# Chunks 0 and 1 of the second mixture by Strassen's products, their first weight combined straight from its loads

## The chip, the cores and the metric

The kernel runs on one core of one Trainium2 chip. The metric is device microseconds of one execution. TensorE (PE) multiplies, VectorE (DVE), ScalarE (ACT) and GpSimd (POOL) do the elementwise work, and SyncE (SP) issues every DMA.

## The reference, cut to what matters

An attention feeds a first channel mixture ("moe"), and that feeds a second one ("moe2"). The change concerns the way from the first mixture to the second and the second's hidden layer:

```python
B, H, S, D = 4, 8, 576, 64                     # 2304 rows of 512 in what follows
x = attention(q, k, v)                         # a band of the scores, plus one on sums of 4 rows
xk, xr = mu_k * x + (1 - mu_k) * x_prev, mu_r * x + (1 - mu_r) * x_prev
k = np.maximum(xk @ w_k, 0.0)                  # 512 x 1024
x1 = sigmoid(xr @ w_r) * (k * k @ w_v)
mu = np.mean(x1, axis=-1, keepdims=True)
var = np.mean((x1 - mu) ** 2, axis=-1, keepdims=True)
xn = (x1 - mu) / np.sqrt(var + 1e-06) * g_ln
out = x1 + np.maximum(xn @ w_ch1, 0.0) @ w_ch2 # 512 x 2048, 2048 x 512
```

The weights arrive as 64-bit floats.

## The kernel before

**Chunks and splits.** The 2304 rows are six chunks of C = 384. Each operand of a large product is split into a high and a low part (`float32r`), and a product is three matmuls (`mm3`, lines 776 to 779): high by high, high by low, low by high.

**Order.** Nothing is issued as it is written down. Each operation is added to a `Plan` with its engine or engines, an assumed cost, a priority and what it reads and writes. `Plan.order` (line 121) is a list scheduler: of what is ready it takes the operation that can start earliest on its engine, and among equals the one with the lowest priority number. Buffers of one tag (a `Buf` with `bufs` slots) are given out in a fixed order of turns, by the first priority of each buffer. The dictionary `PRM` holds the numbers from which the priorities are made. The result is one fixed order for each engine, and SP's order is that of the DMAs.

**Weights.** `load_f32` (line 381) loads a 128x512 piece of 64-bit floats into `w64` (two slots) and makes 32-bit floats of it with two ScalarE operations (lines 393, 395) and two VectorE operations (lines 400, 404) in `wf` (two slots). `load_split` (line 408) adds the copy to the high part and the difference for the low part (line 418). There are 52 such pieces, 16 of `w_ch1` and 16 of `w_ch2` among them.

**Attention.** `attention` (line 451) handles a batch and two heads at a time, 16 units in all; `vsum4` (line 587) makes the sums of four rows of v for twelve of them, by two additions on POOL or one `tensor_reduce` on VectorE. The attention's pool `at` is closed when its last operation is done (`close_att`, `gate`), and the pool `w1tiles` takes its place. Its results stand transposed in `xT[b]`, one for each batch, tag `xT` of `xpool` with two slots.

**First mixture.** For each chunk `prep` (line 784) makes the split xr and xk from `xT` through two slots of `tmu`; `moe_r`, `moe_k` and `accumulate` do the products (tiles `psr`, `psk`, `psv`), and `moe_x` stores x1 to `x1_dram`. Chunk 5's last prep is the last reader of `xT[3]`.

**Second mixture.** Chunks 0 and 1 are done one after the other in the plain form. `c_prep` (line 937) takes one chunk: load x1 into `x1t` (tag `xT` again), statistics, normalised rows `z` stored to `z_dram` one tile of 128 rows after the other, fetched back block by block into `zb` (tag `tmu`, four DMAs each), transposed on VectorE, scaled and split. Chunk 0's is placed in chunk 5 of the first mixture, chunk 1's inside chunk 0's second mixture. `c_h` (line 983) makes the hidden layer from the 16 split pieces of `w_ch1`, which stay in SBUF, four kt by three matmuls for each of 16 f.

Chunks 2 and 3, and 4 and 5, are done as pairs by Strassen's seven products over a 2x2 cut of the rows (the two chunks), of the inner dimension (kt 0, 1 against 2, 3) and of the hidden dimension (f against f + 8). `w1_combine` (line 892) makes the combinations of `w_ch1` from the split pieces and stores them in `s_dram`. `m2_prep` (line 1016) does for both chunks of a pair what `c_prep` does for one, into two buffers `raw0` and `raw1` of the tag `xT`; `m2_split` (line 1095) subtracts and splits for the products in the order of `SEQ`; `m2_product` (line 1125) fetches a combination (`sa`) and runs 2 x 3 matmuls; `m2_h` (line 1153) does the seven for one f, and `m2_acc` the second layer, six row tiles by two pieces of `w_ch2`.

```python
SEQ = (1, 6, 2, 5, 7, 3, 4)
ROW = {1: 0, 6: 5, 2: 2, 5: 1, 7: 4, 3: 3, 4: 2}
for q, (kt, c) in enumerate(((j, 2 * p), (j, 2 * p + 1), (j + 2, 2 * p), (j + 2, 2 * p + 1))):  # m2_prep
minus(C, s(4), s(3), s(1), prio, [(b, 3), (b, 1)], [(b, 4)])
minus(C, s(1), s(1), s(0), prio, [(b, 0)], [(b, 1)])
minus(C, s(5), s(3), s(1), prio, [(b, 3), (b, 1)], [(b, 5)])
```

So product 1 reads row 0 of both `raw` buffers, and product 6 row 5, which is made from rows 0, 1 and 3 of each.

Of the kernel before, what the change touches and what calls it, by code (L numbers as in the profile page):

```python
# [253 lines left out]
def c_pool(n):  # L254
    return 0.2 + n * 0.0028


def c_dma(nbytes, run=2048):

    return nbytes / run * {128: 16, 256: 26, 1024: 72, 1536: 90, 2048: 95, 4096: 220}[run] / 16e3  # L260
# [3 lines left out]
def attn_moe_kernel(  # L264
# [186 lines left out]
    def attention(n, T0, TL):  # L451
# [421 lines left out]

    w1pool = [None]
    w1tiles = lambda: w1pool[0]
    W1, W2 = {}, {}
# [14 lines left out]

    def w1_combine(g, j, prio):

        a = {"11": W1[g, j], "21": W1[g + 2, j], "22": W1[g + 2, j + 2], "12": W1[g, j + 2]}
        to = lambda i, x: s_dram[4 * g:4 * g + 4, SEQ.index(i), :, j, x].rearrange("f p c -> p f c")
        for i, x in ((1, "11"), (2, "12"), (4, "22")):
            for h in range(2):
                b = a[x][h]
                add("SP", c_dma(P * 2048), prio, lambda i=i, h=h, b=b: nc.sync.dma_start(
                    out=to(i, h), in_=b().bitcast(F32).rearrange("p (f c) -> p f c", c=P)),  # L900
                    r=[b], w=[(sd, (i, g, j, h))], lat=2.2)

        def join(x, tag, n):
            hi, lo = a[x]
            o = Buf(wk, [P, 512], F32, tag, n, f"a{x}")
            minus(512, o, lambda: hi().bitcast(F32), lambda: lo().bitcast(F32), prio, [hi, lo], [o], ALU.add)
            return o

        def put(i, src):
            t = Buf(wk, [P, 4, 2, P], F32R, "w64", 2, f"s{i}")  # L910
            part = lambda x: (lambda: t()[:, :, x])
            split(512, part(0), part(1), lambda: src().rearrange("p (f c) -> p f c", c=P), prio, [src], [t])
            add("SP", c_dma(P * 4096), prio, lambda: nc.sync.dma_start(
                out=s_dram[4 * g:4 * g + 4, SEQ.index(i), :, j].rearrange("f p x c -> p f x c"), in_=t().bitcast(F32)),
                r=[t], w=[(sd, (i, g, j, h)) for h in range(2)], lat=2.2)

        a21 = join("21", "wf", 2)
        s1 = join("22", "wf", 2)
        minus(512, s1, a21, s1, prio, [a21], [s1], ALU.add)
        put(5, s1)  # L920
        a11 = join("11", "r", 3)
        minus(512, a21, a11, a21, prio, [a11], [a21])
        put(7, a21)
        minus(512, a11, s1, a11, prio, [s1], [a11])
        put(6, a11)
        a12 = join("12", "wf", 2)
        minus(512, a12, a12, a11, prio, [a11], [a12])
        put(3, a12)

    def c_load(c, prio):  # L930
# [3 lines left out]
            r=[(x1d, c)], w=[(t, i) for i in range(TT)], lat=2.2)  # L934
        return t

    def c_prep(c, x1t, prio):
        mv = Buf(wk, [P, TT, 2], F32, "mv", 2)
        for t in range(TT):
            bs = Buf(wk, [P, 6], F32, "bs", 2)  # L940
# [456 lines left out]
```

## Time and profile before

| | us |
|---|---|
| median of 3 runs (lowest, highest) | 781.41 (779.31, 782.21) |
| profiled execution | 778.78 |
| its span, first to last instruction | 776.8 |
| PE, DVE, ACT, POOL busy | 762.0, 521.8, 396.9, 55.7 |

Attention and first mixture run interleaved until some 265 us, the rest of the first mixture until 383 us, the plain second mixture of chunks 0 and 1 until 517 us, and the two pairs after it to the end. In the rows an operation stands with its line, engine, `out<-in` and shapes; in a timeline the first two numbers are its start and its length in us, and what stands in brackets is how long the engine sat idle before it and what ended that.

### The profile page before, as it was taken

To read this page: it belongs to the slowest core of one execution; us is meant where nothing else is said; L and a number is where in the kernel's file an instruction comes from. 1 tells how busy PE (TensorE), PEld (TensorE's weight loads), DVE (VectorE), ACT (ScalarE), POOL (GpSimd) and SP (SyncE) were. 2 spreads that over 40 slices of the span, in tenths; PEclk is the share of its full clock that TensorE was granted. 3 is DMA by queue.
4 is the path that set the end of the run, shared out by engine and by line. 5 is a ranking of instruction groups with operands and counts; after the bars stand their busy time and mean duration, and the time that the engine had idled before them with its cause. 6 is when DMAs were issued, how large, how long until landed. Compare 5 with 4: busy or idle time off the path is not lost.

```text
span 776.8 us, 15370 instructions
## 1 busy us (share of the span) xinstructions
PE 762.0 (98%) x5859; PEld 659.8 (85%) x5859; DVE 521.8 (67%) x1032; ACT 396.9 (51%) x909; POOL 55.7 (7%) x107
## 2 busy tenths in 40 slices
PE   8999999999999999999999999999999999999998
PEld 5777787878888797988989999999988898989986
DVE  5998999976966669868787857947553365233233
ACT  5888987854756788859655324512331131111110
POOL 2001112211110000000000000200000020000000
PEclk9999999999999999999999999999999999999999
DMA  8999594753320234536564897968763437434422
GB/s 182 183 181 184 150 208 101 140 107 60 86 38 22 96 108 141 173 107 176 161 179 180 245 326 226 285 218 267 189 163 110 121 110 254 153 109 121 123 68 81
DMA packets 182452, 119.10 MB, mean 153 GB/s; under 512 B 125536, under 2 KB 150252, under 8 KB 182380
## 3 DMA queue, kind: packets, MB, share of 16 engines
q1 hardware_dynamic: 182380, 118.14, 56.3%
q8 instruction: 46, 0.75, 0.4%
q14 instruction: 26, 0.21, 0.1%
HBM read 89.26 MB, written 28.84 MB: 152 GB/s over the span
## 4 chain that ended last, share of the span: by engine, by line
PE 86%; DVE 5%; ACT 3%; DMA 3%; issue 1%; SPq 0%; POOL 0%; DVEq 0%; ACTq 0%; POOLq 0%
PE pso L778 9%; PE pso L779 9%; PE pso L777 9%; PE psh L779 8%; PE psh L778 8%; PE psh L777 8%; PE psk L777 4%; PE psv L777 4%; PE psk L779 4%; PE psk L778 4%; PE psv L779 4%; PE psv L778 4%; PE psr L777 2%; PE sc L628 2%; PE pv L747 2%; PE psr L779 2%
## 5 line engine op out<-in xcount | busy, mean ns | idle before, releaser
L778 PE MATMUL psh<-xn,sa 128*128 128x384 f32 x224 | 75.7, 338 | 0.0
L777 PE MATMUL psh<-xn,sa 128*128 128x384 f32 x224 | 75.6, 338 | 0.0
L779 PE MATMUL psh<-xn,sa 128*128 128x384 f32 x224 | 75.5, 337 | 0.0
L777 PEld LDWEIGHTS psh<-xn,sa 128*128 128x128 f32 x224 | 42.1, 188 | 4.5 <-DVE t L1172 0.2
L778 PEld LDWEIGHTS psh<-xn,sa 128*128 128x128 f32 x224 | 42.1, 188 | 3.9
L377 ACT ACTIVATE c22h<-t 128x384 fp32r<-128x384 f32 x16 | 8.4, 526 | 71.4 <-DVE t L1172 71.4
L393 ACT ACTIVATE wf<-w 128x512 f32<-128x512 f32 x52 | 34.8, 669 | 17.0 <-DMA w<-in_moe_w_k_dram 6.2
L400 DVE SCALAR_TENSOR_TENSOR wf<-wf,w 128x512 uint32<-128x512 uint32 x52 | 35.7, 686 | 10.5 <-ACT w L395 9.6
L779 PEld LDWEIGHTS psh<-xn,sa 128*128 128x128 f32 x224 | 42.0, 188 | 0.0
L377 ACT ACTIVATE hh<-psh 128x384 fp32r<-128x384 f32 x32 | 15.7, 492 | 48.8 <-PE psh L779 46.9
L404 DVE SCALAR_TENSOR_TENSOR wf<-w,wf 128x512 uint32<-128x512 uint32 x52 | 35.5, 682 | 0.4
L842 DVE TENSOR_TENSOR kl<-kr,kh 128x384 fp32r<-128x384 f32 x42 | 23.3, 554 | 17.1 <-ACT kr L841 17.1
L395 ACT ACTIVATE w<-w 128x512 uint32<-128x512 uint8 x52 | 34.6, 666 | 0.0
L377 ACT ACTIVATE kr<-psk 128x384 f32<-128x384 f32 x45 | 22.0, 488 | 24.6 <-PE psk L779 21.0
L801 DVE SCALAR_TENSOR_TENSOR tmu<-xT,oms,tmu 128x384 f32<-128x384 f32 (+1 forms) x64 | 31.6, 518 | 0.6 <-ACT tmu L795 0.4
L795 ACT ACTIVATE tmu<-xT,vecs 128x192 f32<-128x192 f32 (+1 forms) x55 | 27.2, 522 | 6.0 <-DVE xrl L805 2.8
L995 DVE SCALAR_TENSOR_TENSOR hl<-psh,hh 128x384 fp32r<-128x384 f32 x32 | 17.7, 555 | 17.1 <-ACT hh L377 16.8
L377 ACT ACTIVATE c11h<-psh 128x384 fp32r<-128x384 f32 x16 | 7.9, 492 | 40.5 <-PE psh L779 40.5
L1149 DVE SCALAR_TENSOR_TENSOR c11l<-psh,c11h 128x384 fp32r<-128x384 f32 x16 | 8.9, 554 | 26.2 <-ACT c11h L377 26.2
L593 DVE TENSOR_REDUCE vd<-v 72x256 f32<-72x1024 f32 x11 | 21.8, 1982 | 6.0 <-PE up L717 6.0
L839 ACT ACTIVATE kh<-kr 128x384 fp32r<-128x384 f32 x48 | 25.0, 521 | 0.8
L431 PE MATMUL warm<-isum,identb 128*128 128x304 bf16 x130 | 23.0, 315 | 1.8 <-DVE identb L324 1.8
(779 smaller groups left out, 2309.0 us busy)
## 6 DMA issues: line engine op xcount, KB each, us to landing
sa<-s_dram SPq DMA_DIRECT2D x112, 256.0 KB
w<-in_moe_w_ch_dram SPq DMA_DIRECT2D x32, 512.0 KB
s_dram<-s SPq DMA_DIRECT2D x16, 512.0 KB
vw<-in_v_dram SPq DMA_DIRECT2D x62, 96.0 KB
x_dram<-r SPq DMA_DIRECT2D x18, 256.0 KB
x1t<-x_dram SPq DMA_DIRECT2D x6, 768.0 KB
z_dram<-x1t SPq DMA_DIRECT2D x18, 256.0 KB
zb<-z_dram SPq DMA_DIRECT2D x96, 48.0 KB
```

The lines of the kernel that those rows point to most:

```text
L377: return [("ACT", c_act(n, True), lambda: nc.scalar.activation(dst(), src(), AF.Relu), False), ("DVE", c_dve(n), lambda: nc.vector.tensor_ ...
L393: add("ACT", c_act(512), prio, lambda: nc.scalar.activation(f(), w64().bitcast(F32)[:, :, 1], AF.Abs, scale=2.0 ** -112), r=[w64], w=[f])
L395: add("ACT", c_act(512), prio, lambda: nc.scalar.activation(w64()[:, :, 0], w64().bitcast(U8).rearrange("p a (b c) -> p a b c", c=4)[:, :, ...
L400: lambda: nc.vector.scalar_tensor_tensor(fu(), fu(), 3, w64()[:, :, 0], op0=ALU.logical_shift_left, op1=ALU.bitwise_or),
L404: lambda: nc.vector.scalar_tensor_tensor(fu(), w64()[:, :, 1], 0x80000000, fu(), op0=ALU.bitwise_and, op1=ALU.bitwise_or),
L777: nc.tensor.matmul(ps, lh, rh, start=start, stop=False, skip_group_check=more)
L778: nc.tensor.matmul(ps, lh, rl, start=False, stop=False, skip_group_check=more)
L779: nc.tensor.matmul(ps, ll, rh, start=False, stop=stop, skip_group_check=more)
L795: add([("ACT", c_act(n, ap=1), lambda t=t, o=o, n=n, cur=cur, kt=kt: nc.scalar.mul(t()[:, o:o + n], cur(), mu[:, kt:kt + 1]), False), ("DV ...
L801: lambda t=t, o=o, n=n, prv=prv, kt=kt: nc.vector.scalar_tensor_tensor(t()[:, o:o + n], prv(), om[:, kt:kt + 1], t()[:, o:o + n], op0=ALU. ...
L839: add("ACT", c_act(C), prio, lambda: nc.scalar.activation(kh(), kr(), AF.Square), r=[kr], w=[kh])
L842: add(either(C, lambda e: e.tensor_tensor(kl(), kr(), kh().bitcast(F32), op=ALU.subtract)), 0, prio, None, r=[kr, kh], w=[kl])
```

## The change

Chunks 0 and 1 become pair 0 of the same form as the other two; `c_load`, `c_prep`, `c_h` and `c_out` go. `m2_prep` and `m2_split` for pair 0 stand in chunk 5 of the first mixture. `w_ch1` no longer stays in SBUF as split pieces: `w1_combine` loads 32-bit pieces, and makes and stores all seven combinations, high and low parts apart. Twelve of the 16 pieces are converted early (`w1_convert`, with priorities in chunks 1 and 2), stored to `w1_dram` and loaded from there; the last four are converted in `w1_combine`. All of `w1_combine` waits for the end of the attention and has priorities in chunk 4. The sums of v get a two-step form on VectorE as well. `w_ch2`'s pieces come in the order 0, 8, 1, 9 and so on. All priorities in `PRM` change; new ones (`ra`, `rb`, `rx`) shift single chunks.

```diff
 PRM = dict(
...
-    d0=190.212, d1=76.663, d2=272.12, d3=80.108, d4=165.422, d5=790.372,
+    d0=235.165, d1=108.349, d2=260.708, d3=463.399, d4=581.694, d5=82886.056,
...
+    wc=10.079, wcs=106.739, wcg=-39.001, p0l=11.872, p0=2.352, p0s=3.263, p0n=7.723, dp=684.729,
+    ra4=-5.44, rb4=10.116, ne=12, we=52.842, wes=25.704, wel=6.378,
...
         def vsum4():
-            def vsum():
-                nc.gpsimd.tensor_tensor(v4()[:, :, 0:2, :], v4()[:, :, 0:2, :], v4()[:, :, 2:4, :], op=ALU.add)
-                nc.gpsimd.tensor_tensor(vd(), v4()[:, :, 0, :], v4()[:, :, 1, :], op=ALU.add)
+            def vsum(e):
+                e.tensor_tensor(v4()[:, :, 0:2, :], v4()[:, :, 0:2, :], v4()[:, :, 2:4, :], op=ALU.add)
+                e.tensor_tensor(vd(), v4()[:, :, 0, :], v4()[:, :, 1, :], op=ALU.add)
-            add([("POOL", c_pool(512) + c_pool(256), vsum, True),
-                 ("DVE", c_dve(1024), lambda: nc.vector.tensor_reduce(
-                     vd(), v4().rearrange("p a r d -> p a d r"), axis=AX.X, op=ALU.add), False)],
+            add([("POOL", c_pool(512) + c_pool(256), lambda: vsum(nc.gpsimd), True),
+                 ("DVE", c_dve(512) + c_dve(256), lambda: vsum(nc.vector), True)],
                 0, pr(0.3), None, r=[v4], w=[v4, vd])
...
+    def w1_parts(g, j):
+        return ("21", g + 2, j), ("22", g + 2, j + 2), ("11", g, j), ("12", g, j + 2)
+    def w1_convert(fo, d, prio):
+        w1_early.add((fo, d))
+        f = Buf(wk, [P, 512], F32, "wf", 2)
+        load_f32(w_ch1[d * P:(d + 1) * P, 512 * fo:512 * fo + 512], f, prio)
+        add("SP", c_dma(P * 2048), prio, lambda: nc.sync.dma_start(out=w1_dram[fo, d], in_=f()),
+            r=[f], w=[(w1d, (fo, d))], lat=2.2)
     def w1_combine(g, j, prio):
-        a = {"11": W1[g, j], "21": W1[g + 2, j], "22": W1[g + 2, j + 2], "12": W1[g, j + 2]}
...
+        for x, fo, d in w1_parts(g, j):
+            a[x] = Buf(w1tiles, [P, 512], F32, "wa", 4, f"a{x}")
+            if (fo, d) in w1_early:
+                add("SP", c_dma(P * 2048), prio - PRM["wel"], lambda x=x, fo=fo, d=d: nc.sync.dma_start(
+                    out=a[x](), in_=w1_dram[fo, d]), r=[(w1d, (fo, d))], w=[a[x]], lat=2.2)
+            else:
+                load_f32(w_ch1[d * P:(d + 1) * P, 512 * fo:512 * fo + 512], a[x], prio)
         def put(i, src):
...
+                tag = f"sa{n_put[0] % 7 + 1}" if g == 0 else f"alt{n_put[1] % 3}"
...
+            add(copy(512, hi, src), 0, prio, None, r=[src], w=[hi])
+            add(either(512, lambda e: e.tensor_tensor(lo(), src(), hi().bitcast(F32), op=ALU.subtract)), 0, prio, None,
+                r=[src, hi], w=[lo])
+            for x, b in enumerate(parts):
+                add("SP", c_dma(P * 2048, 512), prio, lambda x=x, b=b: nc.sync.dma_start(
+                    out=s_dram[4 * g:4 * g + 4, SEQ.index(i), :, j, x].rearrange("f p c -> p f c"),
+                    in_=b().bitcast(F32).rearrange("p (f c) -> p f c", c=P)), r=[b], w=[(sd, (i, g, j, x))], lat=2.2)
...
+        if c == 1:
+            for i in range(PRM["ne"]):
+                g, j = divmod(i // 4, 2)
+                w1_convert(*w1_parts(g, j)[i % 4][1:], start[1] + PRM["we"] + PRM["wes"] * i)
...
-                    W1[g, kt] = load_split(w_ch1[kt * P:(kt + 1) * P, 512 * g:512 * g + 512], 0, f"w1{g}{kt}",
-                                           start[4] + PRM["w1"] + PRM["w1s"] * (4 * g + kt), pool=w1tiles)
+            for i in range(4):
+                w1_combine(i // 2, i % 2, start[4] + PRM["wc"] + PRM["wcs"] * i + PRM["wcg"] * (i > 1))
...
             elif f == PRM["x1"]:
-                x1t[0] = c_load(0, st(TT * 1.33 + 2 * f))
-                xn[0] = c_prep(0, x1t[0], st(TT * 1.33 + 2 * f + PRM["x1d"]))
+                raws = m2_prep(0, T_2 - PRM["p0l"], T_2 - PRM["p0"])
+                xp = m2_split(0, raws, lambda n: T_2 - PRM["p0s"] + PRM["p0n"] * n)
...
-    for c in range(2):
...
-        for f in range(F2 + 2):
-            if f < F2:
-                hs[f] = c_h(c, f, xn[c], st(2 * f))
...
-    for p in range(1, NP):
+    for p in range(NP):
```

## Rows read from the trace of the kernel before

**Rows 1.** The page, busy time of each engine.

```profile
PE 762.0 (98%) x5859; PEld 659.8 (85%) x5859; DVE 521.8 (67%) x1032; ACT 396.9 (51%) x909; POOL 55.7 (7%) x107
```

**Rows 2.** The page, the chain that ended last, by engine.

```profile
PE 86%; DVE 5%; ACT 3%; DMA 3%; issue 1%; SPq 0%; POOL 0%; DVEq 0%; ACTq 0%; POOLq 0%
```

**Rows 3.** Busy time by stage: stretch, its length, then us busy and instructions.

```profile
core 0: us, PE busy (x) PEld busy (x) DVE busy (x) ACT busy (x) POOL busy (x), PEclk, DMA share, GB/s
0.00:60.00 60.00, 54.96 (x961) 41.36 (x964) 48.71 (x108) 43.87 (x120) 9.98 (x38) 1.00 0.93 182
60.00:131.00 71.00, 67.25 (x782) 55.01 (x771) 67.90 (x133) 61.22 (x151) 10.45 (x19) 0.98 0.69 162
131.00:262.00 131.00, 130.05 (x1605) 107.46 (x1604) 101.19 (x210) 86.67 (x234) 18.19 (x37) 1.00 0.38 77
262.00:343.00 81.00, 80.36 (x401) 70.43 (x400) 58.02 (x119) 64.62 (x132) 1.02 (x1) 1.00 0.42 136
343.00:383.00 40.00, 39.41 (x194) 34.70 (x194) 32.21 (x63) 32.05 (x64) 1.02 (x1) 1.00 0.55 158
```

**Rows 4.** Timeline of PE at the start of the plain second mixture and its end.

```profile
381.37 0.39 PE L777 MATMUL psv<-wv5h,kh 128*128 128x512 f32 x1
...
383.45 0.34 PE L777 MATMUL psh<-xnh,w100h 128*128 128x384 f32 x1
...
385.53 0.34 PE L777 MATMUL psh<-xnh,w100h 128*128 128x384 f32 x1
...
517.04 0.34 PE L777 MATMUL psh<-xn,sa 128*128 128x384 f32 x1
```

**Rows 5.** Groups by line and shape: count, us busy, mean ns, idle before.

```profile
L400 DVE SCALAR_TENSOR_TENSOR wf<-wf,w 128x512 uint32<-128x512 uint32 x52 | 35.7, 686 | 10.5 <-ACT w L395 9.6 <-issue 0.3
L393 ACT ACTIVATE wf<-w 128x512 f32<-128x512 f32 x52 | 34.8, 669 | 17.0 <-DMA w<-in_moe_w_k_dram 6.2 <-DMA w<-in_moe_w_ch_dram 5.5 <-DMA w<-in_moe_w_r_dram 3.0
L593 DVE TENSOR_REDUCE vd<-v 72x256 f32<-72x1024 f32 x11 | 21.8, 1982 | 6.0 <-PE up L717 6.0
L890 DVE TENSOR_TENSOR a<-a,a 128x512 f32<-128x512 f32 x14 | 9.6, 684 | 0.2
```

**Rows 6.** Timelines of ACT, DVE and SP where chunk 1's x1t follows chunk 5's prep.

```profile
338.90 0.52 ACT L373 CAST xkh<-tmu 128x384 fp32r<-128x384 f32 x1 [2.58 <-PE psk L779]
...
347.59 0.62 DVE L801 SCALAR_TENSOR_TENSOR tmu<-xT,oms,tmu 128x384 f32<-128x384 f32 x1 [0.20 <-ACT tmu L795]
...
348.23 0.38 SPq L932 DMA_DIRECT2D x1t<-x_dram  x1
...
353.43 1.28 DVE L941 BATCH_NORM_STATS2 bs<-x1t 128x6 f32<-128x512 f32 x2
```

**Rows 7.** Timelines of DVE and SP, the preparation of chunks 4 and 5.

```profile
525.42 1.25 DVE L1027 BATCH_NORM_STATS2 bs<-x1t 128x6 f32<-128x512 f32 x2
...
529.44 0.54 DVE L1049 TENSOR_SCALAR x1t<-x1t,mv,rstd 128x512 f32<-128x512 f32 x1
...
535.75 0.54 DVE L1049 TENSOR_SCALAR x1t<-x1t,mv,rstd 128x512 f32<-128x512 f32 x1
...
544.65 0.54 DVE L1049 TENSOR_SCALAR x1t<-x1t,mv,rstd 128x512 f32<-128x512 f32 x1
...
545.79 0.57 DVE L1065 STREAM_TRANSPOSE raw<-zb 128x384 f32<-128x384 f32 x1
...
547.65 0.56 DVE L1117 TENSOR_TENSOR xn<-raw,xn 128x384 fp32r<-128x384 f32 x1 [0.34 <-ACT xn L373]
...
549.66 4.99 SPq L1061 DMA_DIRECT2D zb<-z_dram  x8
...
554.75 0.89 SPq L1128 DMA_DIRECT2D sa<-s_dram  x2
...
561.55 0.57 DVE L1065 STREAM_TRANSPOSE raw<-zb 128x384 f32<-128x384 f32 x1
...
571.20 0.58 DVE L1065 STREAM_TRANSPOSE raw<-zb 128x384 f32<-128x384 f32 x1 [0.89 <-DMA zb<-z_dram]
```

**Rows 8.** Busy time and granted clock (PEclk) of a stretch after two waits of PE.

```profile
91.00:95.00 4.00, 3.63 (x19) 3.08 (x20) 3.48 (x10) 3.57 (x10) 1.27 (x2) 0.57 0.36 123
```

More of the change, by code (lines that the diff above doesn't have):

```diff
@@ L875, in attn_moe_kernel @@
     w1tiles = lambda: w1pool[0]
-    W1, W2 = {}, {}
+    W2 = {}
     F4 = F2 // 2
@@ L983, in c_h @@
-    def c_h(c, f, xn, prio):
-        hi, lo = xn
-        ps = Buf(ps_k, [P, 512], F32, "pk", 2, "psh")
-        g, o = divmod(f * P, 512)
-        for kt in range(KT):
-            wh, wl = W1[g, kt]
-            add("PE", MM, prio, lambda kt=kt, wh=wh, wl=wl: mm3(
-                ps()[:, :C], wh()[:, o:o + P], wl()[:, o:o + P], hi()[:, kt], lo()[:, kt], kt == 0, kt == KT - 1),
-                r=[(hi, kt), (lo, kt), wh, wl], w=[ps])
-        hh = Buf(wk, [P, C], F32R, "kh", 3, "hh")
-        hl = Buf(wk, [P, C], F32R, "kl", 3, "hl")
-        add(relu(C, hh, lambda: ps()[:, :C]), 0, prio, None, r=[ps], w=[hh])
-        add("DVE", c_dve(C), prio, lambda: nc.vector.scalar_tensor_tensor(
-            hl(), ps()[:, :C], 0.0, hh().bitcast(F32), op0=ALU.max, op1=ALU.subtract), r=[ps, hh], w=[hl])
-        return hh, hl
@@ L999, in c_out @@
-    def c_out(c, pv, load_prio, prio):
-        for t in range(TT):
-            row = c * C + t * P
-            if c == 0:
-                add("DVE", c_dve(512), prio, lambda t=t: nc.vector.tensor_tensor(
-                    x1t[0]()[:, t], pv[t](), x1t[0]()[:, t], op=ALU.add), r=[pv[t]], w=[(x1t[0], t)])
-                add("SP", c_dma(P * 2048), prio, lambda t=t, row=row: nc.sync.dma_start(
-                    out=outf[row:row + P, :], in_=x1t[0]()[:, t]), r=[(x1t[0], t)], lat=2.2)
-                continue
-            x = Buf(wk, [P, 512], F32, "r", 3, "res")
-            add("SP", c_dma(P * 2048), load_prio, lambda row=row, x=x: nc.sync.dma_start(
-                out=x(), in_=x1_dram[row:row + P, :]), r=[(x1d, c)], w=[x], lat=2.2)
-            add("DVE", c_dve(512), prio, lambda t=t, x=x: nc.vector.tensor_tensor(x(), pv[t](), x(), op=ALU.add),
-                r=[pv[t]], w=[x])
-            add("SP", c_dma(P * 2048), prio, lambda row=row, x=x: nc.sync.dma_start(
-                out=outf[row:row + P, :], in_=x()), r=[x], lat=2.2)
+    n_put = [0, 0]
@@ L1253, in attn_moe_kernel @@
     xk[0] = prep(0, "k", prep_prio(T_M + PRM["xk"], PRM["xks"]))
-    x1t, xn = {}, {}
     glb = mub
@@ L1308, in attn_moe_kernel @@
-                xn[0] = c_prep(0, x1t[0], st(TT * 1.33 + 2 * f + PRM["x1d"]))
-        moe_x(c, pvs[c], rr, T + DU + 1)
-    for i, f in enumerate(range(4, F2)):
-        W2[f] = load_split(w_ch2[f * P:(f + 1) * P, :], f, f"w2{f}", T_2 + PRM["w2"] + PRM["w2s"] * i)
-    for kt in range(KT):
-        W1[3, kt] = load_split(w_ch1[kt * P:(kt + 1) * P, 1536:2048], 16 + kt, f"w13{kt}", T_2 + PRM["w13"] + PRM["w13s"] * kt)
-    converted = [b.writer[None] for w in (W1, W2) for hl in w.values() for b in hl]
@@ L1315, in attn_moe_kernel @@
-    for c in range(2):
-        T = T_2 + D2 * c
-        st = lambda i: T + D2 * i / (2 * F2)
-        pv = [Buf(ps_v, [P, 512], F32, f"pv{t}", 1, f"pso{t}") for t in range(TT)]
-        hs = {}
-        if c == 0:
-            x1t[1] = c_load(1, st(PRM["m2l"]))
-            n0 = len(plan.ops)
-            for i in range(4):
-                w1_combine(i // 2, i % 2, T_2 + PRM["wc"] + PRM["wcs"] * i + (30 if i > 1 else 0))
-            for o in plan.ops[n0:]:
-                o.deps.update(converted)
-        for f in range(F2 + 2):
-            if f < F2:
-                hs[f] = c_h(c, f, xn[c], st(2 * f))
-            if f >= 2:
-                accumulate(pv, f - 2, f - 2 == F2 - 1, hs[f - 2], W2[f - 2], st(2 * f + 1))
-            if c == 0 and f == PRM["m2p"]:
-                xn[1] = c_prep(1, x1t[1], st(2 * f))
-        c_out(c, pv, st(2 * F2 - 6), T + D2 + 1)
```

159 lines of the change are left out of this document (51 added, 108 removed).

## The prediction

> **What bounds the kernel now.** I read the busy table first, then the chain of work that ended last, then the busy times by stage. TensorE is busy for 762.0 of 776.8 us [rows 1] and carries 86% of the chain [rows 2]. Busy time flatters a pipelined engine, so the stages say more [rows 3]: from 131 to 383 us TensorE idles for at most 1.5% of any stage, and between 60 and 131 us it idles 71 - 67.25 = 3.75 us while VectorE is busy for 67.90 of 71. That the plain pair after 383 us runs with no gap is worked out below. What the change can win is therefore TensorE work that is taken away, or those few idle microseconds; what it can lose is any new wait of TensorE.
>
> The profiled execution took 778.78 us (776.8 us of span and 2.0 around it), 2.6 us under the median of the three runs (781.41). The sum below is a difference and is added to either.
>
> **Products removed.** In the plain form chunks 0 and 1 take 2 x 16 x 4 x 3 = 384 matmuls of 384 columns for the hidden layer; Strassen's form takes 8 x 7 x 2 x 3 = 336. The second layer keeps its 288 matmuls of 512 columns. Twelve matmuls of 384 columns run from 383.45 to 385.53, 0.173 us each [rows 4]. 48 x 0.173 = **-8.3 us**. The nine of 512 columns before them take 2.08 us, 0.231 each, so the plain pair should last 384 x 0.173 + 288 x 0.231 = 133.1 us, and it lasts 517.04 - 383.45 = 133.6: it runs with no gap, and nothing else is to be had there.
>
> **The weight's path.** Of w_ch1's 16 pieces twelve are converted during the attention, stored, and loaded again; four are converted later. A conversion is two ScalarE passes of 0.67 us and two VectorE passes of 0.68 [rows 5]. Twelve add 16.1 us to ScalarE and 16.4 to VectorE, mostly between 131 and 262 us, where they are busy for 86.7 and 101.2 of 131 [rows 3]: there is cover, and I take +0.5 us. If it failed (the SP queue is in order, and a store waits behind its conversion, holding up the attention loads behind it), TensorE could idle at the rate of 60 to 131 us, 3.75 / 71 = 5%, or 6.9 us; below, a loss of nothing. The combining after the attention is four calls of 4 sums, 7 copies and 7 differences, 44 VectorE operations of 0.684 us if all fall to it [rows 5], 30.1 us, with 28 copies for ScalarE at about the same length, 18.7 us (the copies are an estimate from the 0.67 row); four conversions add 5.5 and 5.4. Out of 262 to 343 us go about 14 conversions with copy and difference (28.7 us of VectorE, 28.1 of ScalarE). VectorE comes to 58.0 + 35.6 - 28.7 = 65 of 81, ScalarE to 64.6 + 24.1 - 28.1 = 61: covered, +0.5 us. The stores and reloads of 256 KB run where the DMA engines are busy for 0.38 to 0.42 of the time; no cost. Later conversions of w_ch2 come out of the plain pair's time, with two due per 15.6 us step; no cost.
>
> **The sum of four rows of v** becomes two additions (512 and 256 elements) in place of one strided reduction that takes 1.98 us, eleven times on VectorE [rows 5]. The two cost at most 2 x 0.684 = 1.37, so at least 0.6 each goes. Four of the eleven lie between 60 and 131 us, where VectorE is full, and shorten what TensorE waits for there; between nothing and all of the 3.75 us I take **-2.5 us**. Here the rule and the row part: the Trainium skill (VectorE: DVE Perf Modes, The perf-mode tier table) gives fp32 tensor_reduce and tensor_tensor the same single rate, by which 1024 elements against 768 would save at most 0.3 us each (an estimate by that page), and this term would be near -1. The row decides.
>
> **The boundary, which I think decides the case.** The plain form needs only chunk 0 normalised and transposed when the second mixture starts; the new form needs both chunks, because product 1 reads a quarter of each half and product 6 a sum of blocks of both chunks. Chunk 1's x1t takes the buffer of xT[3], which is free only when the last prep of chunk 5 has read it. That prep begins when chunk 4's last psk lets xkh go (338.90) and reads xT until 347.59 + 0.62 = 348.2; the load of x1t follows at 348.23 [rows 6], and that order is not changed. The second mixture's turn is at 383.45 [rows 4], 35.2 us later. What must fit in is shown by the next pair's preparation, which does the same steps [rows 6, 7]: load to first statistics 353.43 - 348.23 = 5.2; to the first z 529.44 - 525.42 = 4.0; first z to third, each waiting for the store of the one before, 544.65 - 535.75 = 8.9; to the first fetch back 549.66 - 544.65 = 5.0; to the fifth transpose 561.55 + 0.57 - 549.66 = 12.5 and to the eighth 571.20 + 0.58 - 549.66 = 22.1. After a transpose come scaling, copy and difference, 547.65 + 0.56 - 545.79 - 0.57 = 1.85; product 6 has three subtractions of the same shape (0.56) before its copy as well, so 3.5.
>
> Product 1 needs the fifth transpose (turns of the two fetch buffers go in a fixed order): 348.2 + 5.2 + 4.0 + 8.9 + 5.0 + 12.5 + 1.9 = 385.7, against 384.0 for its second half: it waits 1.7. It ends at 386.2, half of product 6 at 386.7. Product 6 is ready at 348.2 + 23.1 + 22.1 + 3.5 = 396.9: it waits 10.2. Together 11.9. In the rows the SP queue also fetches sa tiles between the z fetches, three times some 0.89 us [rows 7], 2.7 in all; without them 9.2. I take the nearer, **+10.5 us**. The ends: nothing, if the preparation is ordered in a way I do not see; and the pair's preparation as a whole, 571.78 - 525.42 + 5.2 + 3.5 = 55.1 us, against 36.8 until the turn of product 6's second half: +18.3. Nothing covers this wait: before product 1 all of chunk 5 is done, and the second-layer products need the first layer.
>
> After an idle stretch TensorE's clock falls. Between 91 and 95 us, after two waits, the granted clock averaged 0.57 [rows 8], so part of it ran at 1.2 GHz, and 4 x 0.43 = 1.7 us of full speed were lost. I add **+1.6 us** once (ends 0 and twice that).
>
> The Trainium skill speaks for a shorter chain (DMA: Bandwidth & Descriptors, Anatomy of one DMA): 2.0 us and bytes over 436 GB/s, a fit for DMAs from GpSimd, gives 2.6 us for a 256 KB store, where the rows have about 3.9 from one z's end to the next. By that page the wait would be some 3 us shorter.
>
> **Sum:** -8.3 + 0.5 + 0.5 - 2.5 + 10.5 + 1.6 = **+2.3 us**: 781.1 for an execution like the profiled one, 783.7 on the median. A measurement here can tell about 0.5% (3.9 us) from no change; this is 0.3%.
>
> **Rivals.**
> (a) The wait is hidden: chunk 1's preparation ends by its turn. For it: chunk 0's part can be done long before, VectorE has room from 343 to 383 (32.2 of 40). Against it: product 6's chain is 48.7 us by the rows and has 36.8. Then -8.3 + 1.0 - 2.5 = -9.8: 771.6.
> (b) Slower: chunk 1's preparation goes at the pace of the whole pair's. Its place is SP and VectorE between 348 and 400 us, where its steps queue behind w_ch2's conversions and chunk 5's own; its price is +18.3 in place of +10.5, so +10.1: 791.5. It decides once the two waits together pass 12 us (then the sum passes +3.9).
> (c) The early conversions hold up the attention: +6.9 in place of +0.5, and -2.5 not had, with (a)'s boundary: -8.3 + 6.9 + 0.5 = -0.9: 780.5.
> (d) The reduction does not matter to TensorE (-2.5 becomes 0): +4.8, 786.2, counted with the slower part of the forecast.
>
> **Chances.** The forecast, with waits from 6 to 13 us, 0.50: of it 0.34 within 0.5%, 0.14 slower, 0.02 faster. (a) 0.31, nearly all faster. (b) 0.14, slower. (c) 0.05, spread over all three. Together faster 0.35, same 0.36, slower 0.29. The range leaves out the upper half of (b) and the lower end of (a): 769.5 to 790. The likeliest case alone spans 780 to 787.
>
> **What would show it.** In the new profile: some 336 psh matmuls for pair 0 and about 125 us of TensorE work from its product 1 to pair 1's; the reduction replaced by two operations of under 0.7 us; an x1t load of chunk 1 right behind chunk 5's last tmu; TensorE idle between product 1 and product 6 of f = 0 for some 10 us, ended by a copy or difference into xn, with a granted clock under 1 just after. If TensorE runs through that boundary, (a) is right and I am wrong by 12 us; if it idles longer, the z stores and fetches will show which step. If it idles before 262 us more than now, (c) holds.

## The result, and the profile after

The changed kernel takes 771.45 us (median of 4 runs, 770.24 to 774.18) where the kernel before took 780.36 beside it: a ratio of 0.9891, 95% interval 0.9852 to 0.9931. Run again later it gave 773.18 against 779.64: 0.992 (0.9898 to 0.9942). It is faster by 0.8 to 1.1%. I had forecast 783.7 and most of the chance on no change or a loss; rival (a), the hidden wait, is what happened. That its 771.6 lies so close to the median is partly chance: it counts from 781.41, its -2.5 us for the sums of v was not measured, and time that the new pair gave back is not in it.

The page's busy table and chain (shares by engine) of the changed kernel, against [rows 1, 2]:

```profile
PE 753.6 (98%) x5816; PEld 650.2 (84%) x5816; DVE 524.6 (68%) x1083; ACT 398.2 (52%) x916; POOL 63.8 (8%) x113
...
PE 77%; DVE 10%; DMA 6%; ACT 4%; issue 2%; POOL 0%; SPq 0%; DVEq 0%; POOLq 0%; ACTq 0%
```

The records hold 1008 psh matmuls where the kernel before has 1056: the 48 are gone. TensorE's busy time fell by 762.0 - 753.6 = 8.4 us. The span fell from 776.8 to 770.2, by 6.6. VectorE's share of the chain doubled to 10%, a first hint that some of the gain was given back to it.

The boundary is where I expected the loss. Timeline of PE of the changed kernel from the first psh on (start, duration; in brackets the idle time before and what ended it):

```profile
380.44 0.34 PE L778 MATMUL psh<-xn,sa 128*128 128x384 f32 x1
...
382.00 0.39 PE L778 MATMUL psv<-wv6h,kh 128*128 128x512 f32 x1
...
385.88 0.39 PE L780 MATMUL psv<-wv7h,kl 128*128 128x512 f32 x1
386.61 0.44 PE L778 MATMUL psh<-xn,sa 128*128 128x384 f32 x1 [0.34 <-ACT u L371]
...
388.76 0.45 PE L778 MATMUL psh<-xn,sa 128*128 128x384 f32 x1 [0.18 <-DVE u L1097]
```

The two waits come to 0.52 us, where the forecast had 11.9 before it was lowered to 10.5. Neither is ended by an xn: both wait for u, the copy of product 1 and then its sum with product 6. And 18 matmuls of chunk 5's last sums (382.00 to about 386.1) run behind the first nine psh: there was something to cover with. The kernel before had the same 18 behind its first psh, in two groups of nine; the first and the last of them in its timeline:

```profile
387.62 0.40 PE L777 MATMUL psv<-wv6h,kh 128*128 128x512 f32 x1
...
395.77 0.39 PE L779 MATMUL psv<-wv7h,kl 128*128 128x512 f32 x1
```

The next rows say why the preparation was in time. Timelines of SP and DVE of the changed kernel, the x1t of chunks 0 and 1 and chunk 5's last preparation, against [rows 6]:

```profile
304.28 0.46 SPq L957 DMA_DIRECT2D x1t<-x_dram  x1
...
333.37 0.54 DVE L985 TENSOR_SCALAR x1t<-x1t,mv,rstd 128x512 f32<-128x512 f32 x1
...
333.94 0.37 SPq L988 DMA_DIRECT2D z_dram<-x1t  x1
...
336.45 0.36 SPq L957 DMA_DIRECT2D x1t<-x_dram  x1
...
343.11 0.68 DVE L963 BATCH_NORM_STATS2 bs<-x1t 128x6 f32<-128x512 f32 x1
...
344.84 1.13 DVE L802 SCALAR_TENSOR_TENSOR tmu<-xT,oms,tmu 128x384 f32<-128x384 f32 x2
...
348.39 0.55 DVE L985 TENSOR_SCALAR x1t<-x1t,mv,rstd 128x512 f32<-128x512 f32 x1
...
356.08 0.54 DVE L985 TENSOR_SCALAR x1t<-x1t,mv,rstd 128x512 f32<-128x512 f32 x1
...
380.51 0.57 DVE L1001 STREAM_TRANSPOSE raw<-zb 128x384 f32<-128x384 f32 x1
```

Chunk 1 is loaded at 336.45, while chunk 5's preparation still reads xT until 346.0. So it does not take xT's buffer: it takes chunk 0's, whose last z was made at 333.37 and whose store was issued at 333.94. From load to eighth transpose it needs 380.51 + 0.57 - 336.45 = 44.6 us; my steps (5.2 + 4.0 + 8.9 + 5.0 + 22.1) made 45.2. The chain had about the right length and the wrong start, by 348.2 - 336.45 = 11.8 us. The length is partly luck, since single steps were off in both directions: the load to the first statistics took 6.7 us where I had 5.2, on to the first z 5.3 for 4.0, and from first z to third 7.7 for 8.9. The 4.0 was also misread: [rows 7] begin at 525.42, but the first statistics of that pair ran at 522.47, so that the step there took 7.0.

The gain that went missing lies behind that point. Busy times from 383 to 460 us (columns as in [rows 3]), first of the kernel before, then of the changed one:

```profile
383.00:460.00 77.00, 77.00 (x390) 70.07 (x389) 60.93 (x116) 34.02 (x66) 1.62 (x1) 1.00 0.73 214
```

```profile
383.00:460.00 77.00, 74.58 (x367) 65.48 (x365) 60.39 (x123) 34.13 (x68) 5.72 (x5) 1.00 0.86 258
```

TensorE had no idle time there and now has 2.4 us (1.8 when the kernel ran again, busy for 75.24). Its waits in that pair by what ended them, 380 to 460 us, of the changed kernel (total, times, longest); before there is none in this view:

```profile
PE psh L778 <- DVE c L1114: 1.2, 3, 0.6
PE psh L778 <- DVE c L1110: 0.7, 1, 0.7
PE psh L778 <- ACT u L371: 0.3, 1, 0.3
PE psh L778 <- DVE u L1097: 0.2, 1, 0.2
```

And VectorE's own timeline around the last of them, still of the changed kernel:

```profile
450.55 0.58 DVE L1001 STREAM_TRANSPOSE raw<-zb 128x384 f32<-128x384 f32 x1 [1.99 <-DMA zb<-z_dram]
...
458.82 0.58 DVE L1001 STREAM_TRANSPOSE raw<-zb 128x384 f32<-128x384 f32 x1 [2.70 <-DMA zb<-z_dram]
459.32 0.52 DVE L1114 TENSOR_TENSOR c<-psh,u 128x384 f32<-128x384 f32 x1
```

VectorE's order of work is fixed by the plan, and the rows show what that costs. The sum c (L1114) that frees TensorE's bank stands behind a transpose of the second pair's preparation that sat 2.70 us waiting for its fetch, and TensorE's next psh started 459.90, after 0.63 idle. The wait before that, 0.38 us at 443.28, has another cause, since no transpose idled there. The same sum stands behind a conversion of w_ch2, and its load was late; timelines of DVE and ACT:

```profile
441.14 0.69 DVE L402 SCALAR_TENSOR_TENSOR wf<-wf,w 128x512 uint32<-128x512 uint32 x1 [2.53 <-ACT w L397]
...
439.88 0.67 ACT L395 ACTIVATE wf<-w 128x512 f32<-128x512 f32 x1 [3.16 <-DMA w<-in_moe_w_ch_dram]
```

When the kernel ran again that one was the longest, 0.93 us at 445.14 behind a conversion that idled 3.08, and the wait near 460 was not there.

In the plain pair TensorE's bank needed only a relu (on ScalarE or VectorE) and a difference on VectorE per block of the hidden layer; now five of the seven products of a step need a sum on VectorE before their bank is free.

A measure that the experiments share is the time from the first psh to the end of the span. Before it is 776.8 - 383.45 = 393.35; the removed products alone would make it 385.05. In all of these kernels the same 18 matmuls of chunk 5 lie behind the first psh. Each row is one profiled execution.

| kernel | first psh | span | first psh to end |
|---|---|---|---|
| before | 383.45 | 776.8 | 393.35 |
| changed | 380.44 | 770.2 | 389.76 |
| changed, run again | 382.35 | 771.2 | 388.85 |
| chunk 1's load held back | 380.51 | 779.6 | 399.09 |
| product 1 twice | 381.56 | 776.5 | 394.94 |
| all z fetches planned at 5.0 us | 381.65 | 779.8 | 398.15 |
| second pair's z fetches planned at 5.0 us | 378.78 | 766.2 | 387.42 |
| the same, preparation a step later | 380.84 | 768.0 | 387.16 |

Behind the first psh the changed kernels differ almost only in the first pair. From its first output to that of the second pair each of them takes 125.73 us; in VectorE's timeline of the changed kernel:

```profile
509.83 0.69 DVE L1138 TENSOR_TENSOR res<-pso,res 128x512 f32<-128x512 f32 x1 [0.77 <-PE pso L780]
...
635.56 0.69 DVE L1138 TENSOR_TENSOR res<-pso,res 128x512 f32<-128x512 f32 x1 [0.77 <-PE pso L780]
```

### The profile page after: what moved, and what is told of

Its sections match the earlier page's. It is cut to its first block, busy times and chain, and to the rows that moved or that the text cites. A ratio compares the mean times of both kernels' runs of the same rounds, so it can differ in the third digit from the quotient of the medians.

```text
span 770.2 us, 15665 instructions
## 1 busy us (share of the span) xinstructions
PE 753.6 (98%) x5816; PEld 650.2 (84%) x5816; DVE 524.6 (68%) x1083; ACT 398.2 (52%) x916; POOL 63.8 (8%) x113
## 4 chain that ended last, share of the span: by engine, by line
PE 77%; DVE 10%; DMA 6%; ACT 4%; issue 2%; POOL 0%; SPq 0%; DVEq 0%; POOLq 0%; ACTq 0%
PE pso L779 8%; PE pso L778 8%; PE pso L780 8%; PE psh L778 7%; PE psh L779 7%; PE psh L780 7%; PE psk L778 4%; PE psv L778 4%; PE psk L780 3%; PE psk L779 3%; PE psv L779 3%; PE psv L780 3%; DMA w<-in_moe_w_ch_dram 3%; PE warm L433 2%; DVE tmu L802 1%
## 5 line engine op out<-in xcount | busy, mean ns | idle before, releaser
L778 PE MATMUL psh<-xn,sa 128*128 128x384 f32 x336 | 114.0, 339 | 2.4 <-DVE c L1114 1.2
L779 PE MATMUL psh<-xn,sa 128*128 128x384 f32 x336 | 113.6, 338 | 0.0
L780 PE MATMUL psh<-xn,sa 128*128 128x384 f32 x336 | 113.3, 337 | 0.0
L778 PEld LDWEIGHTS psh<-xn,sa 128*128 128x128 f32 x336 | 63.1, 188 | 11.0 <-DVE c L1114 2.1
L779 PEld LDWEIGHTS psh<-xn,sa 128*128 128x128 f32 x336 | 63.1, 188 | 6.1 <-DVE xn L1051 0.2
L780 PEld LDWEIGHTS psh<-xn,sa 128*128 128x128 f32 x336 | 63.1, 188 | 0.0
L379 ACT ACTIVATE c22h<-t 128x384 fp32r<-128x384 f32 x24 | 12.6, 525 | 83.7 <-DVE t L1106 78.6
L402 DVE SCALAR_TENSOR_TENSOR wf<-wf,w 128x512 uint32<-128x512 uint32 x48 | 32.9, 687 | 11.1 <-ACT w L397 10.6
L1083 DVE SCALAR_TENSOR_TENSOR c11l<-psh,c11h 128x384 fp32r<-128x384 f32 x24 | 13.3, 554 | 29.1 <-ACT c11h L379 29.1
L1106 DVE TENSOR_TENSOR t<-psh,t 128x384 f32<-128x384 f32 x24 | 13.3, 554 | 28.5 <-PE psh L780 28.4
L1097 DVE TENSOR_TENSOR u<-psh,u 128x384 f32<-128x384 f32 x24 | 13.3, 555 | 27.2 <-PE psh L780 27.1
L379 ACT ACTIVATE c12h<-c 128x384 fp32r<-128x384 f32 x24 | 12.6, 525 | 37.0 <-DVE c L1110 36.9
L379 ACT ACTIVATE c21h<-c 128x384 fp32r<-128x384 f32 x24 | 12.6, 523 | 34.6 <-DVE c L1114 34.6
L796 ACT ACTIVATE tmu<-xT,vecs 128x384 f32<-128x384 f32 (+1 forms) x51 | 26.8, 539 | 6.9 <-DVE xrl L806 4.0
L1103 DVE TENSOR_TENSOR t<-psh,u 128x384 f32<-128x384 f32 x24 | 13.2, 552 | 20.2 <-PE psh L780 20.1
## 6 DMA issues: line engine op xcount, KB each, us to landing
x1t<-x_dram SPq DMA_DIRECT2D x6, 768.0 KB
```

Source lines behind the costliest of these rows:

```text
L379: return [("ACT", c_act(n, True), lambda: nc.scalar.activation(dst(), src(), AF.Relu), False), ("DVE", c_dve(n), lambda: nc.vector.tensor_ ...
L402: lambda: nc.vector.scalar_tensor_tensor(fu(), fu(), 3, w64()[:, :, 0], op0=ALU.logical_shift_left, op1=ALU.bitwise_or),
L778: nc.tensor.matmul(ps, lh, rh, start=start, stop=False, skip_group_check=more)
L779: nc.tensor.matmul(ps, lh, rl, start=False, stop=False, skip_group_check=more)
L780: nc.tensor.matmul(ps, ll, rh, start=False, stop=stop, skip_group_check=more)
L796: add([("ACT", c_act(n, ap=1), lambda t=t, o=o, n=n, cur=cur, kt=kt: nc.scalar.mul(t()[:, o:o + n], cur(), mu[:, kt:kt + 1]), False), ("DV ...
```

## The experiments

Runs on different chips are compared through their ratios to the kernel before, which ran beside each. The ratio of the changed kernel is taken as 0.992, from the run with more executions; by the 0.9891 of the first run, differences to it that are worked out from ratios would be 2.3 us larger.

**The changed kernel again.** No edit.

> The changed kernel itself once more, beside the kernel before on one chip, to separate what belongs to the kernel from what belongs to an execution. Theory: chunk 0's start (57.3 us in its first profile, 60.1 in that of before) varies by some 2 us between executions, so this profile shows it between 57 and 60.5 us, and the medians stand at a ratio of 0.988 to 0.993. Rival: the earlier start is a property of the changed kernel's priorities, 57 to 58 us again.

773.18 us, ratio 0.992 (0.9898 to 0.9942). The first psr matmul of the kernel before, of the changed kernel, and of this second execution of the changed kernel, one timeline row of each:

```profile
60.15 0.51 PE L777 MATMUL psr<-wr0h,xrh 128*128 128x512 f32 x1
```

```profile
57.31 0.49 PE L778 MATMUL psr<-wr0h,xrh 128*128 128x512 f32 x1
```

```profile
60.12 0.49 PE L778 MATMUL psr<-wr0h,xrh 128*128 128x512 f32 x1
```

The 2.8 us by which the first profile was ahead at chunk 0 belong to the execution (or its chip), not to the change, as the theory had it. Against this profile the span fell by 5.6: 393.35 - 388.85 = 4.5 behind the first psh, and only 1.1 before it.

**Chunk 1's load held back.** A VectorE addition of one column makes chunk 0's x1t live until chunk 5's preparation is done:

```diff
+            if p == 0 and c == 0:
+                held = Buf(wk, [P, 6], F32, "bs", 2, "held")
+                xl = xk[NCH - 1][1]
+                add("DVE", c_dve(1), prio, lambda x1t=x1t, held=held: nc.vector.tensor_tensor(
+                    held()[:, :1], x1t()[:, 0, :1], xl()[:, KT - 1, :1].bitcast(F32), op=ALU.add),
+                    r=[(x1t, 0), (xl, KT - 1)], w=[held])
```

> The changed kernel with chunk 0's x1t buffer held back until chunk 5's preparation has ended (one VectorE addition of a single column that reads both), so that chunk 1's x1t can't take that buffer at 336.45 us. Theory (the forecast failed because chunk 1 was loaded some 11 us earlier than its step assumed): the load falls to about 347, the sums for product 6 are ready 9 to 11 us later than now while its turn stays near 388, TensorE waits 5 to 9 us between 380 and 400, and the kernel takes 776 to 781 us. Rival (the preparation would have been in time from either buffer, because its steps are shorter than my rows): under 2 us more wait, 771 to 774 us.

781.63 us against 778.00: ratio 1.0044 (1.0025 to 1.0063). All of the gain is gone; by the ratio of 0.992 the changed kernel stands at 771.8 on that chip, so the hold costs 9.8 us. Rows of this kernel (its lines below the edit are 6 higher): the load, the waits of TensorE, two stretches with granted clock (PEclk):

```profile
345.59 0.37 SPq L957 DMA_DIRECT2D x1t<-x_dram  x1
```

```profile
PE psh L778 <- ACT xn L375: 4.2, 2, 2.5
PE psh L778 <- DVE u L1103: 1.1, 1, 1.1
PE psh L778 <- ACT u L371: 0.8, 1, 0.8
PE psh L778 <- DVE c L1116: 0.7, 1, 0.7
PE pso L778 <- ACT c11h L379: 0.6, 1, 0.6
PE psh L779 <- DVE xn L1057: 0.2, 1, 0.2
```

```profile
384.90:396.00 11.10, 5.41 (x15) 3.12 (x14) 10.86 (x21) 9.38 (x19) 3.41 (x4) 0.74 0.93 258
396.00:403.00 7.00, 6.23 (x18) 4.25 (x17) 5.30 (x13) 2.98 (x6) 2.00 (x2) 0.68 0.40 140
```

The load moved by 9.1 us and the waits for xn that I had forecast are there. The waits sum to 7.6 us, 5.2 more than in the changed kernel. The rest of the 9.3 to 10.2 us behind the first psh is about what the slow clock costs: 11.1 x 0.26 + 7.0 x 0.32 = 5.1 us of full speed in the two stretches. The theory holds (the time lies just above its 776 to 781 us) and the rival is out, with one reserve: the plan around the boundary moved with the edit, and three psh instead of nine run ahead of the 18 matmuls. Its +3.4 us by the ratio is near the +2.3 that I had predicted, but that is partly chance, since other terms of the sum were off in both directions.

**Product 1 twice** in each step of the first pair:

```diff
-        for j in range(2):
+        for j in (0, 1, 0, 1) if i == 1 and xn is first_pair[0] else (0, 1):
```

> The changed kernel with product 1 of the first pair computed twice in each of the 8 steps (the second result overwrites the first with the same values): 48 matmuls of 384 columns more, as many as the change removed, 8.3 us of TensorE. Theory (some 4.5 us of the 8.3 are given back in the first pair as waits for VectorE): the extra work falls partly into those waits, +4 to +6.5 us, 775 to 778 us, and the waits of psh for VectorE between 400 and 460 us shrink below 1 us in all. Rival (TensorE alone sets the first pair's length, the small waits come from its own results): +8.3 us, 779 to 780.5 us.

777.36 us against 778.00: 0.9994 (0.9981 to 1.0007), 5.6 us over the changed kernel by the ratios, and 5.2 to 6.1 by the measure above. TensorE's waits in the first pair, 380 to 460 us, are now this single row:

```profile
PE psh L778 <- DVE u L1098: 0.6, 1, 0.6
```

Of 8.3 us of work 2 to 3 fell into waits. The time lies in the theory's range, and the waits shrink below 1 us as it said; its premise that 4.5 us are given back as waits was too large.

**Fetches planned later.** The kernel's planner counts a fetch from z as landed 2.2 us after its issue; told 5.0, it puts the transposes later in VectorE's order. First for both pairs:

```diff
-                            "(n p) f -> p n f", p=32)), r=[(zd, (c, t)) for t in range(TT)], w=[(zb, a)], lat=2.2)
+                            "(n p) f -> p n f", p=32)), r=[(zd, (c, t)) for t in range(TT)], w=[(zb, a)], lat=5.0)
```

> The changed kernel, its planner told that the four-part fetches from z land 5.0 us after their issue instead of 2.2, so that it puts VectorE's transposes later in VectorE's order. Theory (in the first pair VectorE's sums stand behind transposes that wait for their fetch, which holds up TensorE): the waits of psh for the sums at about 442 and 459 us (1.35 us together) go, VectorE no longer idles 2 us ahead of a transpose, and the kernel gains 1 to 2 us: 769.5 to 770.5 us. Rival (the waits come from the amount of VectorE's work and not from its order): no gain, 771 to 773 us.

780.32 us, ratio 1.0033 (1.0015 to 1.0051): a miss for both. The edit also reordered the first pair's preparation, whose eighth transpose moved to 394.93 us, and TensorE waited for xn as with the load held back, 4.2 us in two waits. The boundary is closed by a few microseconds only. So the edit was made for the second pair alone (lat=5.0 if p else 2.2):

> The changed kernel with the fetches from z told to the planner as landing after 5.0 us for the second pair's preparation alone, so that the order before about 410 us stays as it is. Theory (VectorE's sums of the first pair stand behind transposes that wait for their fetch): the waits between 440 and 460 us shrink from 1.7 to under 0.6 us and the kernel gains about 1 us. Rival (they come from the amount of VectorE's work): the waits stay in sum, no gain.

769.89 us against 779.64: 0.9882 (0.9857 to 0.9907), 3.3 us below the changed kernel on the same chip; 1.4 of it lies behind the first psh, and chunk 0 happened to start at 57.38. The wait at 459 is gone, and those of psh for c between 380 and 460 us come to 0.4 us. VectorE was busy for 59.63 of the 77 us, hardly less than before the edit (60.86): its order, not its amount of work, made TensorE wait there. The wait behind the late load of w_ch2 went too, so the run does not say which of the two kinds of wait was worth what. By the ratios to the kernel before, the intervals of the two kernels still overlap.

**The same, and the second pair's preparation one step later:**

```diff
-            if f == 1 and p + 1 < NP:
+            if f == 2 and p + 1 < NP:
```

> The changed kernel with the fetches of the second pair's preparation planned at 5.0 us, and that preparation begun one step (some 16 us) later, behind the first conversions of w_ch2 in the second mixture. Theory (between 400 and 415 us VectorE's sums stand behind statistics, the corrections of rstd and conversions that come together): TensorE's loss from 400 to 420 us falls from 1.0 to 1.6 to under 0.5, that from 440 to 460 stays under 0.3, and the kernel is 0.5 to 1 us under the one with the fetch time alone: ratio to before 0.985 to 0.988. Rival (the next boundary turns late, since the second pair's preparation ends 16 us later): TensorE waits some us near 505 us, no gain or a loss.

768.80 us against 778.58: 0.9879 (0.9853 to 0.9905). TensorE's waits in the first pair, all of them, and its busy time in this kernel:

```profile
PE psh L778 <- ACT u L371: 0.3, 1, 0.3
PE psh L778 <- DVE u L1097: 0.2, 1, 0.2
```

```profile
383.00:460.00 77.00, 76.46 (x380) 68.11 (x379) 60.98 (x125) 33.85 (x67) 6.13 (x5) 1.00 0.88 263
```

The waits between 400 and 415 went as expected, and the next boundary was not late. It has the lowest ratio of all these kernels; its interval overlaps that of the changed kernel's second run (0.9898 to 0.9942) by a hair and lies within that of its first (0.9852 to 0.9931), and against the kernel before it with only the fetch time there is no difference that could be told.

**The sums over four rows of v.** The reduction put back:

```diff
-                 ("DVE", c_dve(512) + c_dve(256), lambda: vsum(nc.vector), True)],
+                 ("DVE", c_dve(1024), lambda: nc.vector.tensor_reduce(
+                     vd(), v4().rearrange("p a r d -> p a d r"), axis=AX.X, op=ALU.add), False)],
```

> The changed kernel with the old single reduction for the sums over four rows of v on VectorE (1.98 us where two additions take about 1.2). Theory of the forecast: VectorE ends TensorE's waits between 60 and 131 us, so this costs 1.5 to 2.5 us: 773 to 774 us. Rival (the reduction was off the path, and what was gained before chunk 0 came from other priorities): within 1 us of 771.4.

786.61 us against 778.00, 1.0096 (1.0064 to 1.0128), some 14 us over the changed kernel by the ratios: far outside both. The planner sees another cost and another entry for the port that it has VectorE and POOL share, and orders the whole attention anew, with priorities that were set for the other plan. The run prices a new order, not the instruction. With the cost and the port use of the two additions kept, so that only the instruction differs:

> The changed kernel with the old reduction on VectorE, but planned with the cost and the port use of the two additions, so that every engine's order of work stays as in the changed kernel and only those eight or so instructions differ (1.98 us for about 1.2). Theory (most of the loss of the run before, in which the plan changed too, came from the new order): 1 to 3 us more than the changed kernel. Rival 1 (each reduction delays TensorE by its full difference or more): 5 to 8 us more. Rival 2 (nothing): within 0.7 us.

774.70 us against 773.18 for the changed kernel on the same chip, +1.5, in the theory's 1 to 3; its ratio of 0.9936 (0.9917 to 0.9955) overlaps that of the changed kernel. And the opposite edit to the kernel before, its order kept:

> The kernel before with the two additions in place of the reduction on VectorE, planned with the reduction's cost, so that the order of all work stays as before. The two take 0.73 + 0.42 = 1.15 us by the changed kernel's profile, 0.83 less than the reduction's 1.98, eleven times. Theory (from the reverse edit, which cost 1.3 us): -1 to -2 us, ratio 0.9975 to 0.9987. Rival 1 (the forecast's term): -2.5 us or more. Rival 2: nothing, within 0.5 us.

778.25 against 778.58: 0.9995 (0.9978 to 1.0011), so between -1.7 and +0.9 us. The median fits rival 2, no gain, but the interval does not exclude a gain of 1 to 1.7; rival 1, the forecast's term, is out. The instructions, by line and shape, of the changed kernel and of the one with the reduction in its order:

```profile
L591 DVE TENSOR_TENSOR v<-v 72x512 f32<-72x512 f32 x10 | 7.3, 726 | 0.3 <-DMA v<-in_v_dram 0.3
L592 DVE TENSOR_TENSOR vd<-v 72x256 f32<-72x256 f32 x10 | 4.2, 422 | 0.6
```

```profile
L595 DVE TENSOR_REDUCE vd<-v 72x256 f32<-72x1024 f32 x10 | 20.1, 2007 | 1.0 <-PE up L718 1.0
```

VectorE saves 20.1 - 7.3 - 4.2 = 8.6 us, and the kernel 0.4 to 1.5 us of it by the medians.

**How many of w_ch1's pieces are converted early.** None (ne=0) and all sixteen (ne=16) in place of twelve:

> The changed kernel with none of w_ch1's pieces converted during the attention: all sixteen are converted between 262 and 343 us, where they are combined. It adds 12 x 1.36 = 16.3 us to VectorE and as much to ScalarE in 85 us in which they are busy for 71 and 62 of 88, and takes 12 stores and 12 loads of 256 KB away. Theory (VectorE is then full in that stage): the copies and differences for chunks 3 to 5 come late, TensorE idles 3 to 10 us more between 250 and 383 us, total +3 to +10. Rival (cover enough, and the attention gains VectorE time): within 2 us of the changed kernel.

779.55 us against 779.64: 1.0018 (0.9996 to 1.0039), 6.4 us over the changed kernel on its chip. As the theory said; but TensorE's longest waits are not for VectorE directly. Busy times from 262 to 343 us and TensorE's longest waits from 262 to 383 us, of this kernel:

```profile
262.00:343.00 81.00, 75.00 (x359) 65.38 (x358) 72.42 (x141) 62.26 (x127) 1.50 (x1) 0.98 0.95 300
```

```profile
PE psr L778 <- ACT r L822: 3.1, 1, 3.1
PE psr L778 <- ACT xrh L375: 1.8, 1, 1.8
PE psk L778 <- ACT r L822: 1.6, 1, 1.6
```

The longest wait is for ScalarE, busy for 62 of 81 us: at the start of a chunk the exponential that empties a psr bank stands in its order behind conversions and copies. Two rows of its timeline, one of the copies and that exponential:

```profile
299.11 0.52 ACT L375 CAST xrh<-tmu 128x384 fp32r<-128x384 f32 x1 [1.18 <-DVE tmu L802]
...
305.31 0.57 ACT L822 ACTIVATE r<-psr 128x512 f32<-128x512 f32 x1
```

Copies ahead of it had themselves waited for VectorE's tmu, 2.0 us in three waits from 297 to 303, where VectorE had no idle time. So a full VectorE, as the theory had it, stands behind this wait too.

> The changed kernel with all sixteen pieces of w_ch1 converted during the attention in place of twelve. Theory (the late conversions fill VectorE between 262 and 343 us; each of the twelve moved back cost 0.6 us): four fewer there take up to 1.5 us of TensorE's waits from 255 to 320 us away, total 0 to -1.5. Rival (VectorE is as full before 255 us, and SP holds more waiting stores): TensorE idles 1 to 3 us more between 127 and 255 us.

774.26 us against 778.58: 0.9958 (0.9937 to 0.9979), some 3 us over the changed kernel by the ratios: the theory's gain did not come. Of the rival's loss there is a part: from 127 to 255 us TensorE is busy for 126.38 us, 1.2 less than in the changed kernel run again (127.58). The larger part lies where neither had put it. VectorE has less to do from 262 to 343 us (58.33 in place of 64.09 us), yet TensorE is busy for 76.77 of 81 us in place of 78.75, with two waits of 1.2 and 1.1 us for that same exponential. The plan changed with the number, and this run cannot tell what of the 3 us is order and what is work.

## Why the prediction was wrong, point by point

**Products, -8.3.** Right: the 48 matmuls are gone, with 8.4 us less busy time (7.4 in the second profile). The tally by which I found no gap in the plain pair came out by luck, since its stretch holds 18 psv of chunk 5 and leaves out the pair's last 18 pso; that there was no gap is so all the same (77.00 of 77 us busy from 383 to 460). But I had taken them as time saved in full. 385.05 would have been reached without new waits; the changed kernel has 388.9 to 389.8 from the first psh on and gives 3.8 to 4.7 back. That give-back was no term of my sum: I wrote of w_ch2's conversions "no cost" and never set the five sums on VectorE that each step now needs at once against the second pair's preparation in the same in-order queue. Idle time between 383 and 460 us is 1.8 to 2.4 of it, and the pair form's pace about 0.5: without any wait a pair takes 125.73 us for 124.8 of matmuls counted at the rates of [rows 4], where the plain pair took 133.6 for 133.1. The rest is not placed. The fetch and start edits took 1.4 to 2.6 of it back.

**The weight's path, +1.0.** The early conversions cost TensorE nothing between 131 and 262 us (130.57 of 131 us busy in the second profile against 130.05 [rows 3]; the first has 128.72, with 109 matmul records fewer than the second). From 262 to 343 us it is busy for 78.75 and 78.65 against 80.36 [rows 3]: +1.6 to 1.7 where I had +0.5 for the combining. My test was the stage's mean (VectorE 65 of 81; it was 64.1), which came out right and said too little: the longest wait there, 1.1 us, ends with an exponential that ScalarE starts at 266.15 behind three copies of the combining, 0.6 us each, among its other work.

**The sums of v, -2.5.** Too large: -0.4 measured one way (interval -1.7 to +0.9) and 1.5 the other. I had taken two thirds of TensorE's idle time between 60 and 131 us as ended by these reductions, without a row that showed one ending a wait. In the rows 512 and 256 elements take 0.73 and 0.42 us and 1024 in one strided reduction 2.01, so each exchange saves 0.86 us. The row had the instruction right, and VectorE's time was not the kernel's. The Trainium skill (VectorE: DVE Perf Modes, The perf-mode tier table) gives both operations the same single rate in fp32. These rows do not bear that out for the strided reduction, and that the estimate of near -1 from that rate lies between the two measurements is chance.

**The boundary, +10.5: the step that failed.** "Chunk 1's x1t takes the buffer of xT[3], which is free only when the last prep of chunk 5 has read it" and "that order is not changed": both failed, and the load came at 336.45 in place of 348.2. In the kernel before that was so because the other buffer, chunk 0's x1t, served as the residual of chunk 0's output in the plain form until that was done. The change drops that use with the plain form's c_out: m2_out reads its residuals again from x1_dram, so chunk 0's buffer comes free with its last z, at 333.4. The rows of before could not show it; the diff did, in the lines that it removes. With the buffer held back the rest of the step came true: waits for xn, and 9.8 us against the 12.1 of this term and the clock's together. "Nothing covers this wait" was wrong as well: [rows 4] begin with psv matmuls ahead of the first psh, and I did not ask whether others follow it. Eighteen do, 4.1 us, and they did in the kernel before.

**The clock, +1.6.** No idle stretch, no loss: the granted clock stays 1.00 from 383 to 460 us. Under the forecast's premise the term was too small and the wait too large: with the load held back about 5 us were waits and 4 to 5 the slow clock, 10 together where I had 10.5 + 1.6.

**Not separated.** From chunk 0's start to the first psh the changed kernel gained 1.1 us net in the second profile, though the combining cost 1.6. So some 2.7 were gained elsewhere ahead of it; the sums of v account for about one. Much of it lies between 60 and 131 us, where TensorE's idle time fell from the 3.75 of [rows 3] to 1.53 (69.47 busy) and the granted clock rose from 0.98 to 1.00; with the reduction put back and the order kept it is 2.25 (68.75 busy). So of the 2.2 us less idle time there the sums of v account for about 0.7. That this comes near the -2.5 of my term is chance. The rest is left to the new order of the attention, which no run here took apart.

## What to carry to other kernels

Where a transfer waits for a buffer, ask which buffer it will get in the new kernel, and look for it in the lines that the change removes: a tile whose last use is deleted comes free early, and no trace of the old kernel shows that. When products are traded for sums on an in-order engine, count what else stands in that engine's order, above all instructions that may wait for a DMA; planning the fetches of the second pair later took 1.4 to 2.3 us back here, while VectorE's work stayed almost the same. Price an instruction with the order of all work kept, for in a planned kernel a changed cost moves everything else.

## Not expected of the hardware

Two additions of 512 and 256 elements took 0.73 + 0.42 us, one reduction of the same 1024 through a strided view 2.01. With the load held back, TensorE waited 2.5, 0.8 and 1.7 us within 9 us; the granted clock averaged 0.74 over the 11.1 us that hold these waits and 0.68 over the next 7, so that it stood partly at 1.2 in place of 2.4 GHz, and that cost about as much as the waits. And chunk 0 of one and the same program started at 57.31 us in one execution and 60.12 in another, which may have run on another chip, so two profiles have to be compared from an event in the middle.
